# Tails of the output product in pairs, a residual on GpSimd, and tails of w2's transposed product two chunks at a time

## The chip, the cores and the metric

The kernel runs on one core of one Trainium2 chip. The metric is device time in microseconds (us), the median of several executions. A core has a matrix engine (TensorE, "PE" in the profile, with its weight loads as "PEld"), a vector engine (VectorE, "DVE"), an activation engine (ScalarE, "ACT"), a general engine (GpSimd, "POOL") and SyncE ("SP"), which here only issues DMAs. Each engine works through its own instruction list in order; semaphores tie the lists together. DMAs are issued from a queue of SP, ACT or POOL, and a DMA that must wait holds up what stands behind it on that queue. Data lies in SBUF (128 partitions) and, for matmul results, in PSUM, of which the kernel uses eight banks of 128 x 512 float32.

## The reference

The forward pass is a linear-attention block and a gated MLP, each with a layer norm ahead of it and a residual; the program returns the result and the gradients of the input and of five weights. S = 2048 rows, D = 640, 32 heads of 20, hidden size F = 1728. In short:

```python
h  = x + attention(layernorm(x), wqkv, wo)      # linear attention, phi(t) = elu(t) + 1
xn = layernorm(h)
gate = xn @ w1 ;  up = xn @ w3                  # 640 -> 1728
hh = silu(gate) * up
h2 = h + hh @ w2                                # output 0
# backward, from the given gradient g of h2:
ghh = g @ w2.T                                  # 640 -> 1728
g_up, g_gate = ghh * silu(gate), ghh * up * silu'(gate)
grad_w2 = hh.T @ g                              # and so on for w1, w3, wo, wqkv, x
```

All inputs and outputs are bfloat16; products add up in float32.

## The kernel before

F = 1728 is 13 chunks of 128 columns and a tail of 64: `FT = 14`, `FL = 64`. The 2048 rows are handled in `SC = 4` chunks of `W = 512`, each of `TPC = 4` row tiles of 128; `HD = 320` is half of D.

The program runs attention first, then the MLP stage, then the gradient of w2 and the rest of the backward pass. The change touches the MLP stage, and a mask that attention uses.

**The loop of the MLP stage.** For chunk `c` and hidden chunk `fc`, `mlp(c, fc, between)` issues, in this order: five matmuls of 128 x 512 of w2's transposed product for the position two ahead (`mlp_ghh`, `ghh_chunk`, L398 for the tail and L386 through `mm5_to` else); five matmuls of w1 (`gp`); ACT's two sigmoids (L772, L773); five matmuls of w3 (`upp`); ACT's copies of both to SBUF (L779, L783). The copy of L783 needs its `gate` buffer to be free, so the store that reads the buffer's former contents must have landed. At `fc = 13`, where only 64 columns are left of both, `gp` holds w1's and w3's tail together. Two hidden chunks make a pair. `mlp_pair` puts seven VectorE operations of 128 x 1024 on a list, `later` (L808): gate×sig, then hhT, then s2, gate×ghh, two on s2, ghh. Their results go to DRAM: hhT from SP's queue (`hh_d`), the other two from POOL's (`gg_d`, L791). `drain` takes one at a time off the list, four times for each `fc`.

**The tail of w2's transposed product.** At `fc = 13` of the product (issued at `fc = 11` of the loop) the stationary operand has 64 columns. The tail of a chunk is computed as two column halves of the array, one for each 256 rows of the chunk: 10 matmuls of 64 columns by 256 in one PSUM bank, copied by ACT in two steps.

**The output product.** `o2_steps(c)` is a generator: 8 accumulations (4 row tiles, 2 halves of D) of 14 matmuls of 128 x 320 each, L833, 112 in all. The last one of each has 128 rows in the contraction like the others; its lower 64 rows of w2 are zeros (a memset on GpSimd, L881). It yields after each 7 or 8 matmuls. The loop of chunk `c + 1` takes one step for each `fc`; VectorE adds h to each half (L838). Chunk 3's own product runs after the loop, with one entry of `later` drained at each step, and its results are stored from ACT's queue. The next stage's first loads (`load_hh(0)`) and the gradient of w2 (L1025, its tail of column halves L1011) follow.

**The residual.** `f2_at(t)` computes h for row tile `t`: five matmuls of 128 x 320 for each half (L642) and the addition of x. In tiles 5 to 7 (and in the second halves of 0 to 3) TensorE does the addition: one more matmul with the identity (L640), then ACT copies the sum to `x_sb` (L647). Elsewhere VectorE adds from PSUM. `ln2.part` then takes VectorE's statistics of the half (L147), and `f2_hn` normalizes: VectorE's small operations (L150, L153), a power on GpSimd (L154), and a VectorE operation of 128 x 640 (L160). Tiles 4 to 15 are made during chunks 0 to 2, one chunk ahead of their use: tiles 5, 6 and 7 in chunk 0.

**The mask.** `make_mask` fills a block-diagonal mask of 128 x 5 x 7 x 20 with a VectorE memset and two GpSimd selects for each block row; `masked` multiplies by it.

Of the kernel before, what the change touches and what calls it, by code (L numbers as in the profile page):

```python
# [9 lines left out]
P = 128  # L10
# [45 lines left out]
def kernel(  # L56
# [136 lines left out]
    load_x(3, 4)  # L193
    load_x(4, 8)

    mask = cp.tile([P, DT, M_MAX, DH], BF16, name="mask")

    def make_mask(m):
        a, b = M_H[m]
        v = mask[:, m, 0:b - a, :]  # L200
        V.memset(v, 1.0)

        G.affine_select(out=v, in_=v, pattern=[[-DH, b - a], [0, DH]], compare_op=ALU.is_ge, fill=0.0,
                        base=m * P - a * DH, channel_multiplier=1)
        G.affine_select(out=v, in_=v, pattern=[[DH, b - a], [0, DH]], compare_op=ALU.is_gt, fill=0.0,
                        base=a * DH + DH - m * P, channel_multiplier=-1)

    def masked(out, acc, m):

        a, b = M_H[m]  # L210
        V.tensor_tensor(out=out[:, m, a * DH:b * DH].rearrange("p (h e) -> p h e", e=DH),
                        in0=acc.rearrange("p (h e) -> p h e", e=DH), in1=mask[:, m, 0:b - a, :], op=ALU.mult)


    w1 = U2.tile([P, DT, FP], BF16, name="w1", tag="A")
# [171 lines left out]
                     stop=(c == DT - 1))  # L387
        return acc

    def ghh_chunk(n, acc):  # L390

        c, fc = divmod(n, FT)
        if fc == FT - 1:
            gh, hw = ghh[n // 2], W // 2
            G.memset(gh[FL:, 1, :], 0.0)
            for d in range(DT):
                for h in range(2):
                    T.matmul(acc[h * FL:(h + 1) * FL, 0:hw], lhsT=w2T[:, d, fc * P:fc * P + FL],  # L398
                             rhs=g2T[c][:, d, h * hw:(h + 1) * hw], start=(d == 0), stop=(d == DT - 1))
            for h in range(2):  # L400
                A.copy(out=gh[:FL, 1, h * hw:(h + 1) * hw], in_=acc[h * FL:(h + 1) * FL, 0:hw])
            return
        mm5_to(acc, w2T, fc, g2T[c])
# [111 lines left out]
    for t in range(ST):  # L515
        first = None
        if t < RAW:
            first = phi_tiles()
            kh = [ps.tile([P, 512], F32, name="k0", tag="m", bufs=2) for _ in range(2)]

            def act(i, j):
                A.activation(first[i][:, j * HD:(j + 1) * HD], kh[j][:, 0:HD], (AF.Exp, AF.Relu)[i],
                             scale=ln1.rs[:, t:t + 1])

            def between():
                act(0, 0)
                p1_tr(t + 1)
                act(1, 0)
            k = p1_mm(t, D, between, kh)
            act(0, 1)  # L530
            act(1, 1)
        else:
            k = p1_mm(t, D, (lambda: p1_tr(t + 1)) if t + 1 < XT_DMA else None)
        steps = v_steps.get(t, (R,) * len(held))
        for step in steps:
            if step is R:
                held.pop(0)()
            elif step[0] in V_OPS:
                V_OPS[step[0]](step[1])
        phi(k, pk_all[:, t, :], t, first)  # L540
        for when in ("A", "B", "L"):
            for step in steps:
                if step is not R and step[0] == when:
                    p1_norm(step[1])
            if when == "A" and t in QT:
                q_tile(QT.index(t))
        if 3 <= t < 7:
            ghh_chunk(t - 3, ps.tile([P, 512], F32, name="gp", tag="m", bufs=2))
# [80 lines left out]
    ps = pool("pap", space=PSUM)  # L629
    hn, hnT, hhT = {}, {}, {}  # L630

    at_rest = []

    def f2_at(t, tag="at", halves=(0, 1), hold=False):
        for j in halves:
            on_pe = t < 2 * TPC and (t > TPC or (t < TPC and j == 1))
            at = ps.tile([P, 512], F32, name="at", tag=tag, bufs=2)
            xs = x_sb[:, t, j * HD:(j + 1) * HD]
            if on_pe:
                T.matmul(at[:, 0:HD], lhsT=ident[:], rhs=xs, start=True, stop=False)  # L640
            for c in range(DT):
                T.matmul(at[:, 0:HD], lhsT=pqT[:, c, t * P:(t + 1) * P], rhs=Wp[:, c, j * HD:(j + 1) * HD],  # L642
                         start=(c == 0 and not on_pe), stop=(c == DT - 1))

            def rest(at=at, xs=xs, j=j, on_pe=on_pe):
# [109 lines left out]

    def mlp_ghh(n):
        if n < SC * FT:
            ghh_chunk(n, ps.tile([P, W], F32, name="mm", bufs=4))

    AHEAD = 2  # L760

# [36 lines left out]
    def drain(n):  # L798
        for _ in range(min(n, len(later))):
            later.pop(0)()  # L800

    def mlp_pair(c, k, sig, s2, gate, up, gh):

        hh = hhT[c][:, 2 * k:2 * k + 2, :]

        def op(out, a, b, alu=ALU.mult, to=None, r0=0, q=dma):
            def go():
                V.tensor_tensor(out=out, in0=a, in1=b, op=alu)  # L808
                if to is not None:
                    store(to, r0, c, k, out, q)  # L810
            later.append(go)

        sig, s2, gate, up, gh = (x[:] for x in (sig, s2, gate, up, gh))
        op(gate, gate, sig)
        op(hh, gate, up, to=hh_d)
        op(s2, gate, s2)
        op(gate, gate, gh, to=gg_d, r0=F, q=dmaG)
        op(s2, s2, sig, ALU.add)
        op(s2, s2, up)
        op(gh, s2, gh, to=gg_d, q=dmaG)  # L820

    def o2_steps(c, q=dma, tag="o2"):

        jobs = [(i, j, fc) for i in range(TPC) for j in range(2) for fc in range(FT)]
        o2 = {}
        stops = [n * 15 // 2 - 1 for n in range(1, FT)]
        for n, (i, j, fc) in enumerate(jobs):
            if fc == 0:
                o2["ps"] = ps.tile([P, 512], F32, name="o2", tag=tag, bufs=2)
                if j == 0:  # L830
                    t = c * TPC + i
                    o2["sb"] = x_sb[:, t, :] if c == SC - 1 else pf.tile([P, D], BF16, name="h2", bufs=2)[:]
            T.matmul(o2["ps"][:, 0:HD], lhsT=hhT[c][:, fc, i * P:(i + 1) * P],  # L833
                     rhs=w2[:, fc, j * HD:(j + 1) * HD], start=(fc == 0), stop=(fc == FT - 1))
# [43 lines left out]
    pa = pool("pa", "right")  # L878

    w2 = U1.tile([P, FT, D], BF16, name="w2", tag="D")  # L880
    G.memset(w2[64:, FT - 1, :], 0.0)  # L881

    def sides(c):
        side = ({}, {})
# [32 lines left out]
    for c in range(SC):  # L917
# [9 lines left out]
        for fc in range(FT):  # L927
# [15 lines left out]
            if c == 2 and fc == 3:  # L943
# [26 lines left out]
            dmaT(out=hb[b][:, :, a:a + n], in_=hh_d[f0 + a:f0 + a + n, :])  # L970

    load_hh(0)
    for _ in o2_steps(SC - 1, A.dma_start, "at"):
        drain(1)
    pa.release()
    ph.release()
# [166 lines left out]
    def q_parts():  # L1143
# [6 lines left out]
        for m, t0, j in order:  # L1150
# [6 lines left out]
            if (t0, j) == (8, 1):  # L1157
                a, b = M_H[m]
                A.copy(out=two(qp[:, m, :]), in_=acc[m][:, :, 0:HD])
                V.tensor_tensor(out=gz8[:, m, 0:b - a], in0=acc.pop(m)[:, 1, HD + a:HD + b], in1=mask[:, m, 0:b - a, 0],  # L1160
                                op=ALU.mult)
                dmaT(out=QT[:, :, m * P:(m + 1) * P], in_=qp[:, m, :])
            yield
# [343 lines left out]
```

## Time and profile before

| what | value |
|---|---|
| median of 3 runs | 823.68 us (823.57 to 823.91) |
| the profiled execution's span | 821.9 us |
| MLP stage, chunks 0 to 3 and the last output product | about 97 to 342 us of the span |
| TensorE's granted clock | 9 tenths or more in each of 40 slices |
| DMA | 157.26 MB, mean 191 GB/s |

The times are taken around the program, the span is from its first to its last instruction as the hardware profiler saw it; 1.8 us lie between the two. The page's second part cuts the span into 40 slices and prints the busy tenths of each engine:

```profile
PE   8999999999999999999999999999999999999998
PEld 6677544555555555777777777767777777555554
DVE  7869887999898566300057777772681545200000
ACT  7856688665565666011122212222212334211111
POOL 2243333323223212100001111110220000000000
PEclk9999999999999999999999999999999999999999
DMA  9999889696485556999677897258984898885771
```

A slice is 20.5 us. TensorE is busy from end to end; VectorE is nearly as busy as TensorE in slices 5 to 12, which are the MLP stage, and GpSimd has room everywhere.

### The profile page before, as it was taken

To read this page: it belongs to the slowest core of one execution; us is meant where nothing else is said; L and a number is where in the kernel's file an instruction comes from. 1 tells how busy PE (TensorE), PEld (TensorE's weight loads), DVE (VectorE), ACT (ScalarE), POOL (GpSimd) and SP (SyncE) were. 2 spreads that over 40 slices of the span, in tenths; PEclk is the share of its full clock that TensorE was granted. 3 is DMA by queue.
4 is the path that set the end of the run, shared out by engine and by line. 5 is a ranking of instruction groups with operands and counts; after the bars stand their busy time and mean duration, and the time that the engine had idled before them with its cause. 6 is when DMAs were issued, how large, how long until landed. Compare 5 with 4: busy or idle time off the path is not lost.

```text
span 821.9 us, 14179 instructions
## 1 busy us (share of the span) xinstructions
PE 814.4 (99%) x5522; PEld 522.6 (64%) x5549; DVE 453.1 (55%) x961; ACT 325.0 (40%) x609; POOL 133.1 (16%) x194
## 2 busy tenths in 40 slices
PE   8999999999999999999999999999999999999998
PEld 6677544555555555777777777767777777555554
DVE  7869887999898566300057777772681545200000
ACT  7856688665565666011122212222212334211111
POOL 2243333323223212100001111110220000000000
PEclk9999999999999999999999999999999999999999
DMA  9999889696485556999677897258984898885771
GB/s 233 254 279 227 207 234 312 196 242 157 145 213 155 166 181 162 250 241 267 195 170 179 206 204 188 70 113 178 268 216 93 164 200 181 201 199 137 165 170 38
DMA packets 320883, 157.26 MB, mean 191 GB/s; under 512 B 238704, under 2 KB 314064, under 8 KB 320816
## 3 DMA queue, kind: packets, MB, share of 16 engines
q1 hardware_dynamic: 278768, 115.54, 61.3%
q0 software_dynamic: 7328, 24.48, 8.9%
q10 hardware_dynamic: 34720, 16.34, 8.7%
q8 instruction: 43, 0.70, 0.4%
q14 instruction: 24, 0.20, 0.1%
HBM read 47.01 MB, written 51.13 MB: 119 GB/s over the span
## 4 chain that ended last, share of the span: by engine, by line
PE 94%; DVE 2%; ACT 1%; DMA 1%; issue 0%; SPq 0%; POOL 0%; DVEq 0%; ACTq 0%
PE mm L386 20%; PE job L1271 20%; PE ghn L1070 14%; PE gxn L1429 8%; PE o L833 7%; PE gw L1025 7%; PE gwo L1155 3%; PE big L266 3%; PE gr L1127 3%; PE dkv L1375 3%; PE macc L416 2%; PE at L642 2%; DMA wqkv<-in_A_wqkv_dram 1%; PE dkv L1303 1%; DVE st L147 1%; DMA Wp<-pkx 1%
## 5 line engine op out<-in xcount | busy, mean ns | idle before, releaser
L1271 PE MATMUL job<-gb,hnN 128*128 128x432 bf16 (+2 forms) x656 | 117.0, 342 | 0.0
L1070 PEld LDWEIGHTS <-ggb 128*128 128x128 bf16 x864 | 84.5, 98 | 32.8
L1271 PEld LDWEIGHTS <-hnN 128*128 128x128 bf16 x656 | 63.6, 98 | 53.4
L386 PE MATMUL mm<-pqT,w 128*128 128x512 bf16 x397 | 93.1, 379 | 0.5
L386 PEld LDWEIGHTS <-w 128*128 128x128 bf16 x540 | 52.5, 98 | 63.1 <-issue 0.8
L1275 ACT CAST obs<-job 128x432 bf16<-128x432 f32 (+3 forms) x61 | 29.3, 480 | 123.1 <-PE job L1271 123.1
L833 PE MATMUL o<-w,hhT 128*128 128x320 bf16 x448 | 67.7, 299 | 0.1
L1070 PE MATMUL ghn<-w13a,ggb 128*128 128x320 bf16 x448 | 63.5, 299 | 0.0
L1070 PE MATMUL ghn<-w13b,ggb 128*128 128x320 bf16 x416 | 61.4, 299 | 0.0
L386 PE MATMUL mm<-g2T,w2T 128*128 128x512 bf16 x227 | 58.5, 379 | 0.6
L833 PEld LDWEIGHTS <-hhT 128*128 128x128 bf16 x448 | 43.8, 98 | 23.8 <-issue 0.2
L1025 PE MATMUL gw<-g,hb 128*128 128x320 bf16 x416 | 56.8, 299 | 0.0
L1135 POOL TENSOR_TENSOR sz<-Zb,g_h 128x640 f32<-128x640 bf16 x16 | 20.2, 1260 | 198.8 <-DVE g_h L1133 107.7
L1025 PEld LDWEIGHTS <-hb 128*128 128x128 bf16 x416 | 40.6, 98 | 16.0 <-issue 0.3
L1429 PE MATMUL gxn<-wqT,gT 128*128 128x320 bf16 x320 | 48.7, 299 | 0.0
L406 ACT CAST ghh<-mm 128x512 bf16<-128x512 f32 x48 | 28.3, 590 | 44.7 <-PE mm L386 39.0
L772 ACT ACTIVATE sig<-mm 128x512 bf16<-128x512 f32 x56 | 33.9, 605 | 25.1 <-PE mm L386 21.6
L1082 ACT ACTIVATE gs<-ghn 128x640 bf16<-128x640 f32 x16 | 11.2, 703 | 78.9 <-PE ghn L1070 73.4
L386 PEld LDWEIGHTS <-w2T 128*128 128x128 bf16 x260 | 25.4, 98 | 23.3
L266 PEld LDWEIGHTS <-pqT 128*128 128x128 bf16 x320 | 30.6, 98 | 14.4 <-issue 1.7
L1429 PEld LDWEIGHTS <-gT 128*128 128x128 bf16 x320 | 31.3, 98 | 12.2
L266 PE MATMUL big<-wqkv,pqT 128*128 128x320 bf16 x250 | 38.5, 299 | 0.3
(210 smaller groups left out, 1282.3 us busy)
## 6 DMA issues: line engine op xcount, KB each, us to landing
hh_d<-hhT SPq DMA_DIRECT2D x24, 256.0 KB, 2.8
gg_d<-gate POOLq DMA_DIRECT2D x24, 256.0 KB, 4.1
gg_d<-ghh POOLq DMA_DIRECT2D x24, 256.0 KB, 3.5
ggb<-gg_d SPq DMA_DIRECT2D x6, 896.0 KB, 5.4
ggb<-gg_d ACTq DMA_DIRECT2D x6, 832.0 KB, 5.7
out_dram<-obs ACTq DMA_DIRECT2D x39, 108.0 KB, 3.0
x_sb<-in_A_x_dram SPq DMA_DIRECT2D x6, 640.0 KB, 5.4
ggb<-gg_d SPq DMA_DIRECT2D x2, 1728.0 KB, 13.5
```

The lines of the kernel that those rows point to most:

```text
L266: T.matmul(acc, lhsT=pqT[:, c, t * P:(t + 1) * P], rhs=wqkv[:, c, n0:n0 + HD], start=(c == 0), stop=(c == DT - 1))
L386: T.matmul(acc[:], lhsT=w[:, c, fc * P:(fc + 1) * P], rhs=rhs[:, c, :], start=(c == 0), stop=(c == DT - 1))
L406: A.copy(out=ghh[n // 2][:, n % 2, :], in_=acc[:])
L772: A.activation(sig[:, i, :], gp[:], AF.Sigmoid)
L833: T.matmul(o2["ps"][:, 0:HD], lhsT=hhT[c][:, fc, i * P:(i + 1) * P], rhs=w2[:, fc, j * HD:(j + 1) * HD], start=(fc == 0), stop=(fc == FT - 1))
L1025: T.matmul(acc[:, j, 0:HD], lhsT=hb[b][:, t, i * P:(i + 1) * P], rhs=g2[:, t, j * HD:(j + 1) * HD], start=(t == 0), stop=(t == ST - 1))
L1070: T.matmul(acc[:, j, 0:HD], lhsT=ggb[t // 2][:, k, lo:lo + P], rhs=rhs[:, j * HD:(j + 1) * HD], start=(k == 0), stop=(k == NG - 1))
L1127: T.matmul(gr[t][:, j, 0:HD], lhsT=ghT[t][:, c, :], rhs=wT2[:, c, j * HD:(j + 1) * HD], start=(c == 0), stop=(c == DT - 1))
L1155: T.matmul(acc[m][:, j, 0:n], lhsT=r_sb[:, t, m * P:(m + 1) * P], rhs=g_hx[:, t, j * HD:j * HD + n], start=(t == 0), stop=(t == ST - 1))
L1271: T.matmul(acc[:, 0:n], lhsT=lhs[:, t, m * P:(m + 1) * P], rhs=rhs(t), start=(t == 0), stop=(t == ST - 1))
L1275: A.copy(out=ob, in_=acc[:, 0:n])
L1429: T.matmul(acc[:, j, 0:HD], lhsT=g, rhs=wqT[:, k, j * HD:(j + 1) * HD], start=(k == 0), stop=(k == 14))
```

## The change

It has four parts.

1. *Tails of w2's transposed product.* An even chunk computes its own tail and that of the next chunk in one group of 20 matmuls into one PSUM bank; ACT copies the second half to a new tile, `ght2`, from which the odd chunk's two copies read.
2. *Residual of tiles 5, 6 and 7.* The six identity matmuls go. ACT copies the product to a float32 tile `xa`, GpSimd adds x (two additions of 128 x 320 a tile, on the queue that also issues the `gg_d` stores and the power), and the statistics are held back until the end of that `fc`, behind one more drained VectorE operation.
3. *Output product of chunks 2 and 3* (`o2_pairs`). Row tiles `i` and `i + 2` of one half of D share the last step: the tail's 64 contraction rows of tile `i` stand in partitions 0 to 63, those of `i + 2` in 64 to 127, so w2's tail is loaded a second time to the upper partitions (a load of 80 KB more, and the memset goes), and hhT's tail of the last 256 rows is copied there by a DMA of 64 x 256 on SP's queue, as an eighth entry of the list `later`. Tile `i` ends with its tail; tile `i + 2` begins with it. Chunk 2 does this in two groups of four tails, chunk 3 in one group of eight with all eight PSUM banks. The steps yield after each 8 of the 104 full matmuls, so there are 13 yields.
4. *Mask.* It has one element for each head, and `masked` reads it with a broadcast along the 20 columns.

```diff
-    def ghh_chunk(n, acc):
+    def ghh_chunk(n, new_acc):
...
-            for d in range(DT):
+            if c % 2 == 0:
+                src = new_acc()
+                for k in range(2):
+                    for d in range(DT):
+                        for h in range(2):
+                            T.matmul(src[h * FL:(h + 1) * FL, k * hw:(k + 1) * hw], lhsT=w2T[:, d, fc * P:fc * P + FL],
+                                     rhs=g2T[c + k][:, d, h * hw:(h + 1) * hw], start=(d == 0), stop=(d == DT - 1))
+                ghh["next"] = pf.tile([P, hw], BF16, name="ght2")
+            else:
+                src = ghh["next"]
...
+            if c % 2 == 0:
+                A.copy(out=ghh["next"][:], in_=src[:, hw:2 * hw])
...
-            on_pe = t < 2 * TPC and (t > TPC or (t < TPC and j == 1))
+            on_pe = t < TPC and j == 1
+            on_pool = TPC < t < 2 * TPC
...
+                if on_pool:
+                    xa = pf.tile([P, HD], F32, name="xa", tag="h2", bufs=2)
+                    A.copy(out=xa[:], in_=at[:, 0:HD])
+                    G.tensor_tensor(out=xs, in0=xa[:], in1=xs, op=ALU.add)
+                    st_later.append(lambda: ln2.part(x_sb, t, j))
+                    return
...
         op(hh, gate, up, to=hh_d)
+        if c >= SC - 2 and k == FT // 2 - 1:
+            later.append(lambda: dma(out=hh[FL:, 1, W // 2:], in_=hh[:FL, 1, W // 2:]))
...
+    def o2_pairs(c, groups, q):
...
+        def main(i, j, first):
+            for fc in range(lo):
+                T.matmul(accs[i, j][:, 0:HD], lhsT=hhT[c][:, fc, i * P:(i + 1) * P],
+                         rhs=w2[:, fc, j * HD:(j + 1) * HD], start=(first and fc == 0), stop=(not first and fc == lo - 1))
+                done[0] += 1
+                if done[0] % 8 == 0:
+                    yield
...
+        for low, tags in groups:
+            for (i, j), tag in zip(low, tags):
+                acc_of(i, j, tag)
+                yield from main(i, j, True)
+            for (i, j), tag in zip(low, tags[len(low):]):
+                acc_of(i + 2, j, tag)
+                js = slice(j * HD, (j + 1) * HD)
+                for k, first in ((i, False), (i + 2, True)):
+                    r0 = FL * first
+                    T.matmul(accs[k, j][:, 0:HD], lhsT=hhT[c][r0:r0 + FL, lo, k * P:(k + 1) * P],
+                             rhs=w2[r0:r0 + FL, lo, js], start=first, stop=not first)
+            for i, j in low:
+                end(i, j)
+            for i, j in low:
+                yield from main(i + 2, j, False)
+                end(i + 2, j)
...
+        if c == SC - 2:
+            yield from o2_pairs(c, [([(i, 0), (i, 1)], ["o2", "o2", "at", "at"]) for i in range(2)], q)
+            return
+        if c == SC - 1:
+            yield from o2_pairs(c, [([(i, j) for i in range(2) for j in range(2)],
+                                     ["at", "at", "o2", "o2", "mm", "mm", "mm", "mm"])], q)
+            return
...
-    G.memset(w2[64:, FT - 1, :], 0.0)
...
             drain(1)
+            stats_held()
...
-                    dma(out=w2[0:FL, FT - 1, :], in_=B_w2[(FT - 1) * P:F, :])
+                    for r0 in (0, FL):
+                        dma(out=w2[r0:r0 + FL, FT - 1, :], in_=B_w2[(FT - 1) * P:F, :])
```

More of the change, by code (lines that the diff above doesn't have):

```diff
@@ L194 @@
     load_x(4, 8)
-    mask = cp.tile([P, DT, M_MAX, DH], BF16, name="mask")
+    mask = cp.tile([P, DT, M_MAX], BF16, name="mask")
     def make_mask(m):
         a, b = M_H[m]
-        v = mask[:, m, 0:b - a, :]
+        v = mask[:, m, 0:b - a]
         V.memset(v, 1.0)
-        G.affine_select(out=v, in_=v, pattern=[[-DH, b - a], [0, DH]], compare_op=ALU.is_ge, fill=0.0,
+        G.affine_select(out=v, in_=v, pattern=[[-DH, b - a]], compare_op=ALU.is_ge, fill=0.0,
                         base=m * P - a * DH, channel_multiplier=1)
-        G.affine_select(out=v, in_=v, pattern=[[DH, b - a], [0, DH]], compare_op=ALU.is_gt, fill=0.0,
+        G.affine_select(out=v, in_=v, pattern=[[DH, b - a]], compare_op=ALU.is_gt, fill=0.0,
                         base=a * DH + DH - m * P, channel_multiplier=-1)
@@ L211, in masked @@
         V.tensor_tensor(out=out[:, m, a * DH:b * DH].rearrange("p (h e) -> p h e", e=DH),
-                        in0=acc.rearrange("p (h e) -> p h e", e=DH), in1=mask[:, m, 0:b - a, :], op=ALU.mult)
+                        in0=acc.rearrange("p (h e) -> p h e", e=DH), in1=mask[:, m, 0:b - a].unsqueeze(2).to_broadcast([P, b - a, DH]),
+                        op=ALU.mult)
     w1 = U2.tile([P, DT, FP], BF16, name="w1", tag="A")
@@ L395, in ghh_chunk @@
             G.memset(gh[FL:, 1, :], 0.0)
-            for d in range(DT):
-                for h in range(2):
-                    T.matmul(acc[h * FL:(h + 1) * FL, 0:hw], lhsT=w2T[:, d, fc * P:fc * P + FL],
-                             rhs=g2T[c][:, d, h * hw:(h + 1) * hw], start=(d == 0), stop=(d == DT - 1))
+            if c % 2 == 0:
[8 more added lines that the diff above has]
+                src = ghh["next"]
             for h in range(2):
-                A.copy(out=gh[:FL, 1, h * hw:(h + 1) * hw], in_=acc[h * FL:(h + 1) * FL, 0:hw])
+                A.copy(out=gh[:FL, 1, h * hw:(h + 1) * hw], in_=src[h * FL:(h + 1) * FL, 0:hw])
+            if c % 2 == 0:
+                A.copy(out=ghh["next"][:], in_=src[:, hw:2 * hw])
             return
-        mm5_to(acc, w2T, fc, g2T[c])
+        acc = mm5_to(new_acc(), w2T, fc, g2T[c])
         if n % 2 == 0:
@@ L547 @@
         if 3 <= t < 7:
-            ghh_chunk(t - 3, ps.tile([P, 512], F32, name="gp", tag="m", bufs=2))
+            ghh_chunk(t - 3, lambda: ps.tile([P, 512], F32, name="gp", tag="m", bufs=2))
         m_part(0, M0.get(t, ()))
@@ L630, with stats_held @@
     hn, hnT, hhT = {}, {}, {}
-    at_rest = []
+    at_rest, st_later = [], []
+    def stats_held():
+        while st_later:
+            st_later.pop(0)()
     def f2_at(t, tag="at", halves=(0, 1), hold=False):
         for j in halves:
-            on_pe = t < 2 * TPC and (t > TPC or (t < TPC and j == 1))
+            on_pe = t < TPC and j == 1
+            on_pool = TPC < t < 2 * TPC
             at = ps.tile([P, 512], F32, name="at", tag=tag, bufs=2)
@@ L643, in f2_at, with rest @@
                          start=(c == 0 and not on_pe), stop=(c == DT - 1))
-            def rest(at=at, xs=xs, j=j, on_pe=on_pe):
+            def rest(at=at, xs=xs, j=j, on_pe=on_pe, on_pool=on_pool):
+                if on_pool:
[4 more added lines that the diff above has]
+                    return
                 if on_pe:
@@ L757, in mlp_ghh @@
         if n < SC * FT:
-            ghh_chunk(n, ps.tile([P, W], F32, name="mm", bufs=4))
+            ghh_chunk(n, lambda: ps.tile([P, W], F32, name="mm", bufs=4))
     AHEAD = 2
@@ L820, in mlp_pair, with acc_of, end, o2_steps @@
         op(gh, s2, gh, to=gg_d, q=dmaG)
-    def o2_steps(c, q=dma, tag="o2"):
+    def o2_pairs(c, groups, q):
+        accs, done, sb = {}, [0], {}
+        lo = FT - 1
+        def acc_of(i, j, tag):
+            accs[i, j] = ps.tile([P, 512], F32, name="o2", tag=tag, bufs=4 if tag == "mm" else 2)
+        def main(i, j, first):
[5 more added lines that the diff above has]
+                    yield
+        def end(i, j):
+            t, js = c * TPC + i, slice(j * HD, (j + 1) * HD)
+            if c == SC - 1:
+                sb[i] = x_sb[:, t, :]
+            elif j == 0:
+                sb[i] = pf.tile([P, D], BF16, name="h2", bufs=2)[:]
+            V.tensor_tensor(out=sb[i][:, js], in0=accs.pop((i, j))[:, 0:HD], in1=x_sb[:, t, js], op=ALU.add)
+            if j == 1:
+                q(out=out0S[:, t, :], in_=sb[i])
+        for low, tags in groups:
[14 more added lines that the diff above has]
+                end(i + 2, j)
+    def o2_steps(c, q=dma):
+        if c == SC - 2:
+            yield from o2_pairs(c, [([(i, 0), (i, 1)], ["o2", "o2", "at", "at"]) for i in range(2)], q)
+            return
+        if c == SC - 1:
+            yield from o2_pairs(c, [([(i, j) for i in range(2) for j in range(2)],
+                                     ["at", "at", "o2", "o2", "mm", "mm", "mm", "mm"])], q)
+            return
         jobs = [(i, j, fc) for i in range(TPC) for j in range(2) for fc in range(FT)]
@@ L828, in o2_steps @@
             if fc == 0:
-                o2["ps"] = ps.tile([P, 512], F32, name="o2", tag=tag, bufs=2)
+                o2["ps"] = ps.tile([P, 512], F32, name="o2", bufs=2)
                 if j == 0:
-                    t = c * TPC + i
-                    o2["sb"] = x_sb[:, t, :] if c == SC - 1 else pf.tile([P, D], BF16, name="h2", bufs=2)[:]
+                    o2["sb"] = pf.tile([P, D], BF16, name="h2", bufs=2)[:]
             T.matmul(o2["ps"][:, 0:HD], lhsT=hhT[c][:, fc, i * P:(i + 1) * P],
@@ L972 @@
     load_hh(0)
-    for _ in o2_steps(SC - 1, A.dma_start, "at"):
+    for _ in o2_steps(SC - 1, A.dma_start):
         drain(1)
@@ L1159, in q_parts @@
                 A.copy(out=two(qp[:, m, :]), in_=acc[m][:, :, 0:HD])
-                V.tensor_tensor(out=gz8[:, m, 0:b - a], in0=acc.pop(m)[:, 1, HD + a:HD + b], in1=mask[:, m, 0:b - a, 0],
+                V.tensor_tensor(out=gz8[:, m, 0:b - a], in0=acc.pop(m)[:, 1, HD + a:HD + b], in1=mask[:, m, 0:b - a],
                                 op=ALU.mult)
```

## The prediction

> **What bounds the kernel now.** I read the page's first part (busy time by engine), then its chain of waits, then the windows and the timelines of the places that the change touches.
>
> ```profile
> PE 814.4 (99%) x5522; PEld 522.6 (64%) x5549; DVE 453.1 (55%) x961; ACT 325.0 (40%) x609; POOL 133.1 (16%) x194
> ...
> PE 94%; DVE 2%; ACT 1%; DMA 1%; issue 0%; SPq 0%; POOL 0%; DVEq 0%; ACTq 0%
> ```
>
> TensorE is busy for 99% of the span and is 94% of the chain. So a matmul taken away is worth its own pitch at once, and a wait put in front of a matmul costs its whole length. The averages hide how near the other engines are, so I cut the MLP stage into windows (start and end; length; busy us of PE, PEld, DVE, ACT, POOL with instruction counts; PE clock; DMA share; GB/s):
>
> ```profile
> 110.00:120.00 10.00, 9.95 (x51) 4.99 (x51) 8.86 (x17) 6.66 (x13) 5.05 (x7) 1.00 0.90 254
> 158.00:203.50 45.50, 45.29 (x255) 24.53 (x258) 44.16 (x95) 25.41 (x48) 14.39 (x20) 1.00 0.72 199
> 324.00:331.00 7.00, 6.97 (x52) 4.91 (x51) 5.80 (x12) 2.25 (x4) 1.29 (x3) 1.00 0.46 151
> ```
>
> The clock is 1.00, TensorE has no gap worth a name. In chunk 0 (first row) DMA is at 0.90; in chunk 1 (second) VectorE is at 44.16 of 45.50, so it can hardly give way. Whatever the change makes late shows on TensorE only where the slack runs out; I look for those places.
>
> **Part 1, matmuls taken away.** Prices: an output-product matmul of 320 columns is 0.136 us (2.04/15 in the chain), one of 512 columns 0.216 us (5 between 322.90 and 323.98). A group of 64-column tails (rows of the timeline and of the chain: start, us, engine, what, count; later also idle time and its releaser):
>
> ```profile
> 130.31 2.32 PE L386 MATMUL mm<-pqT,w 128*128 128x512 bf16 x10
> 132.56 0.74 PE L398 MATMUL mm<-g2T,w2T 128*64 128x256 bf16 x10
> ...
> 203.51 2.04 PE o L833 x15
> ...
> 394.97 2.29 PE gt L1011 x32
> ```
>
> Ten matmuls from 130.31 end at 132.47, the group starts at 132.56 and the next matmul follows at 133.23: 0.67 for five pairs of 0.108 (256 columns), so about 0.1 before and 0.1 behind, 0.2 a group. L1011 shows that column halves run in pairs: 32 in 2.29, 0.14 a pair.
> - w2's transposed product: the same matmuls in two groups instead of four: 2 × 0.2 = −0.40.
> - Residual: six identity matmuls of row tiles 5, 6, 7 go: 6 × 0.136 = −0.82.
> - Output product's tails: no row of before has two 64-*row* halves together. Lower bound of the gain: they run one by one, the count stays 16, and three switches of 0.2 are paid: +0.6. Upper: pairs at no switch: 8 × 0.136 = −1.09. I take pairs with a switch of 0.2 a group, as for column halves, the nearest row. Chunk 3: 8 × 0.136 = 1.09 becomes 4 × 0.14 + 0.2 = 0.76; chunk 2, twice: 0.54 becomes 0.48. Sum −0.45.
>
> Together −1.67. The Trainium skill ("TensorE: Matmul & The Clock Gate", Part 3) states that matmuls in different row groups start a few ns apart and run at once, which is the value taken; no run here shows it yet.
>
> **Part 2, what is hidden.** The mask of 7 instead of 140 elements a partition: GpSimd's selects stand before its 7.67 us of idle time ahead of 57.03, so nothing is gained; the broadcast operand keeps VectorE's element count. Taken 0, bounds −0.1 and +0.2 (one masked product, 0.3 us, late by half). The extra w2 load (80 KB) and the two SBUF copies of hhT's last 64 rows (64x256) are on SP's queue, behind the hh_d stores and ahead of later out_0 stores; the copy is wanted 52 matmuls, 7.1 us, after chunk 3's product begins, against 3.9 us from issue to landing for the hh_d stores (median of the DMA issues between 100 and 160). Taken 0, bounds 0 and +0.3. The two ACT copies more are 0.4 each (two 128x320 in 0.76 at 120.19) where ACT is 56% busy (25.41/45.50): 0. The memset of w2's pad (0.62 on POOL): 0.
>
> **Part 3, the end of chunk 3's loop.** The steps of the output product end after 8 instead of 7 or 8 matmuls, so the step after the loop has no matmul left. Between the last gate product and the first matmul that needs the last pair's hhT stood 22 + 12 = 34 matmuls, 4.62 us; now 8 + 12 = 20, 2.72 us. What they cover:
>
> ```profile
> 322.90 1.24 PE L386 MATMUL mm<-hnT,w 128*128 128x512 bf16 x5
> ...
> 324.18 0.60 ACT L772 ACTIVATE sig<-mm 128x512 bf16<-128x512 f32 x1 [1.04 <-PE mm L386]
> 325.87 0.58 ACT L783 CAST gate<-mm 128x512 bf16<-128x512 f32 x1
> ...
> 326.49 0.69 DVE L808 TENSOR_TENSOR gate<-gate,sig 128x1024 bf16<-128x1024 bf16 x1 [1.02 <-ACT gate L783]
> 327.21 0.69 DVE L808 TENSOR_TENSOR hhT<-gate,up 128x1024 bf16<-128x1024 bf16 x1
> ```
>
> The gate product ends at 323.98, hhT at 327.90: 3.92 later, all of it a chain ACT, ACT, DVE, DVE that the change leaves alone. Matmul 13 waits 3.92 − 2.72 = 1.20. One matmul on, (0,1) takes the PSUM tile that chunk 2's last tile leaves, and that addition (0.44) now stands right behind hhT on VectorE: 327.90 + 0.44 = 328.34, 4.36 behind 323.98, against 2.72 + 1.20 + 0.14 = 4.06: another 0.30. Before paid 0.06 there (gap at 330.96). Sum +1.44; bounds 1.2 (only the first wait) and 2.1 (one more VectorE operation of 0.69 between).
>
> **Part 4, GpSimd's additions in chunk 0.** Price: two in 1.53, so 0.765 each, against nothing on VectorE before (TensorE added).
>
> ```profile
> 63.60 1.53 POOL L358 TENSOR_TENSOR pr<-hx,Zb 128x320 f32<-128x320 bf16 x2 [1.26 <-DVE rden L365]
> ...
> 110.06 0.71 POOL L791 DMA_DIRECT2D gg_d<-ghh  x1 [1.03 <-DVE ghh L808]
> 110.28 0.88 DVE L147 BATCH_NORM_STATS2 st<-x_sb 128x6 f32<-128x320 bf16 x2
> 113.06 0.69 DVE L808 TENSOR_TENSOR gate<-gate,ghh 128x1024 bf16<-128x1024 bf16 x1
> 114.30 0.74 POOL L791 DMA_DIRECT2D gg_d<-gate  x1 [1.68 <-ACT up L779]
> 119.71 0.58 ACT L783 CAST gate<-mm 128x512 bf16<-128x512 f32 x1 [2.61 <-DMA gg_d<-gate]
> 121.13 1.24 PE L386 MATMUL mm<-g2T,w2T 128*128 128x512 bf16 x5
> ```
>
> Tile 5: the additions stand on POOL behind the issue that ends at 110.77, so they end at 112.30; the two statistics wait for them on VectorE and end near 112.8, not 111.16. hhT goes ahead of them now, but behind them stand the norm's small operations, GpSimd's power (0.88 from 111.74), hn that waits for it, and gate×ghh behind hn: 113.06 + 1.64 = 114.7, with rounding 114.4 to 114.9: +1.35 to +1.85, and with it the issue at 114.30. Who waits: ACT's gate copy at 119.71 (its buffer is read by that store, idle 2.61), which frees at 120.29 the PSUM tile that TensorE wants at 121.13. Slack 0.84, of which 0.54 goes since TensorE comes four identity matmuls earlier: 0.30. So a stall of 1.05 to 1.55, with up to 0.3 behind it at the next up product: 1.85 at most. At the least 0: this store took 5.35 from issue to landing, the median of all gg_d stores is 4.1, and 1.35 − 1.25 is under the slack; against it, the median between 100 and 160 is 5.3. Taken the middle, +0.95. Tiles 6 and 7 have 1 to 4 us of slack at each wait. Chunk 1's VectorE (1.34 idle, less 0.66 of TensorE time gone there): 0, upper bound +0.5.
>
> A rule speaks against this part: the Trainium skill ("SBUF — State Buffer", Who interferes with whom) has GpSimd and VectorE lock one port pair for a whole instruction when VectorE has two SBUF inputs. Its sign is in the trace: a 640-wide scalar operation took 1.86 at 60.67 beside GpSimd products, and 0.32 alone at 75.92. By the rule six additions could hold VectorE 6 × 0.765 = 4.6 us more, and the sum would rise by up to that, less what VectorE's idle times in the chunk (1.59, 0.71, 1.37, 1.74 behind 110) take; by the order used here VectorE stands in the statistics meanwhile, one input each, and nothing is added.
>
> **Sum.** −1.67 + 1.44 + 0.95 = +0.72 against the profiled 821.9, so 822.6. The median, 823.68, is 1.8 above that span (time around it, unchanged): 824.4.
>
> **The rivals.**
> - *Cover holds*: the store lands at the median time, no stall in chunk 0. For it: landings differ by over 1 us. 823.68 − 1.67 + 1.44 = 823.45; with tails at no switch (−0.64) and 1.2 at the loop's end, 822.6; and if the chain at 323.98 were shorter too, under 822.0. Against: the chain is ACT and DVE time, not DMA.
> - *VectorE held by GpSimd (slower)*: in chunk 0 each addition stretches a VectorE operation, as 1.86 for 0.32 at 60.67. For it: VectorE 8.86 of 10.00 busy there; against: the order puts it in the statistics. From 114.9 on, each us of lateness of gate×ghh goes one to one to TensorE, from 0.9 on the time is over 825.33; with two of the six stretched by 1.5, 824.4 + 0.9 to 2.4: 825.4 to 826.8.
> - *Row halves run one by one*: +0.6 in place of −0.45: 824.4 + 1.05 = 825.5. The change then doesn't do what it says. Only the column halves of L1011 speak against it.
>
> **Numbers.** A measurement of this kernel tells 0.2% (1.65 us) from no change, so "same" is 822.03 to 825.33. Likeliest 0.52 (its own range 823.5 to 825.3), cover holds 0.25 (0.10 of it under 822.03), held VectorE 0.15, one by one 0.08 (half under 825.33). Faster 0.10; slower 0.15 + 0.04, and 0.03 for the likeliest's upper bounds: 0.22; same 0.68. Range 822.3 to 826.0: some 0.07 are left out below and 0.1 above.
>
> **What would show it.** Right: no identity rows of tiles 5 to 7; two L398-like groups of 20; the four pairs of chunk 3 in some 0.55 us; TensorE waits of 1.2 and 0.3 behind the last gate product, released by DVE; ACT's wait for gg_d<-gate near 120 longer by over 1 us, TensorE idle behind it. Wrong: no gap at the loop's end (another order on DVE); tail pairs at 0.27 each; VectorE operations of over 1 us in chunk 0; TensorE gaps between 158 and 203 (VectorE has become the bound).

## The result and the profile after

The changed kernel takes 827.11 us (median of 5 runs, 825.62 to 828.34) against 823.68 us before; the ratio is 1.0036, with a 95% interval of 1.0024 to 1.0048. Measured once more beside other kernels it took 826.11 against 823.80, ratio 1.0022 (1.0010 to 1.0034). It is slower, by 3.4 and 2.3 us between the medians, and both medians lie above the forecast range of 822.3 to 826.0, the second by 0.1.

The page of the changed kernel, busy time by engine and the shares of the chain of waits:

```profile
PE 813.6 (99%) x5516; PEld 521.0 (63%) x5543; DVE 454.2 (55%) x961; ACT 324.9 (39%) x611; POOL 135.3 (16%) x199
...
PE 84%; DVE 8%; DMA 3%; issue 3%; ACT 1%; POOL 1%; SPq 0%; DVEq 0%; POOLq 0%; ACTq 0%
```

TensorE has less to do (813.6 for 814.4), and the span is longer (824.8 for 821.9). VectorE is now 8% of the chain, DMA 3%: TensorE waits. Where, the windows tell (start and end; length; busy us of PE, PEld, DVE, ACT, POOL with instruction counts; PE clock; DMA share; GB/s). Before:

```profile
125.00:158.00 33.00, 32.79 (x172) 16.40 (x175) 28.27 (x53) 26.11 (x50) 10.73 (x16) 1.00 0.91 269
...
324.00:345.00 21.00, 20.97 (x155) 14.99 (x154) 10.36 (x20) 2.25 (x4) 2.96 (x6) 1.00 0.94 216
```

After:

```profile
125.00:158.00 33.00, 31.11 (x166) 15.32 (x168) 27.44 (x51) 23.80 (x48) 12.94 (x19) 1.00 0.88 263
158.00:203.00 45.00, 44.50 (x245) 24.18 (x248) 43.90 (x96) 26.11 (x50) 13.91 (x21) 1.00 0.77 201
324.00:345.00 21.00, 19.81 (x140) 12.86 (x138) 13.30 (x24) 4.41 (x8) 3.64 (x6) 1.00 0.77 174
```

TensorE stands still for 1.9 us in the rest of chunk 0 (33.00 − 31.11) and for 1.2 us at the end of chunk 3. A finer account comes from the start times of the same matmuls in two traces. The table gives how much later they start than before, in the first profile of the changed kernel and in that of its second measurement:

| matmul | start before | first | second |
|---|---|---|---|
| residual product, tile 0, second half | 90.27 | +0.72 | −0.05 |
| residual product, tile 7 | 124.5 | +0.11 | −0.58 |
| residual product, tile 8 (chunk 1) | 157.8 | +2.75 | +1.79 |
| residual product, tile 11 | 191.62 | +3.20 | +2.27 |
| residual product, tile 12 (chunk 2) | 218.1 | +2.42 | +1.49 |
| residual product, tile 15 | 256.2 | +2.42 | +1.49 |
| gradient of w2, first | 342.37 | +3.08 | +2.15 |

The first row is a wait for a DMA transpose in attention (1.10 us at 31.99). The changed kernel's second profile doesn't have it, and of the kernels below only the one without the residual has it (1.28), so it isn't counted to the change. From tile 0 to tile 7 five of the six identity matmuls are won; the sixth (0.14) stands behind that row. Between tiles 7 and 8 stand +2.64 and +2.37; 0.55 of it is chunk 1's tails, done early, and the sixth identity matmul, which is gone there, hides 0.14 of waits: 2.2 and 2.0 are waits. Chunk 1 adds 0.45, its missing tail group gives 0.78 back, and from tile 15 to the end stands +0.66, the last cover against the gains of chunks 2 and 3.

The timeline of the changed kernel, chunk 0 (start, us, engine, what, count, idle before and its releaser):

```profile
111.10 2.41 DVE L828 TENSOR_TENSOR hhT<-gate,up 128x1024 bf16<-128x1024 bf16 x1
113.43 0.87 DVE L147 BATCH_NORM_STATS2 st<-x_sb 128x6 f32<-128x320 bf16 x2
116.15 0.68 DVE L828 TENSOR_TENSOR gate<-gate,ghh 128x1024 bf16<-128x1024 bf16 x1
...
111.49 1.46 POOL L663 TENSOR_TENSOR x_sb<-xa,x_sb 128x320 bf16<-128x320 f32 x2
117.13 0.74 POOL L811 DMA_DIRECT2D gg_d<-gate  x1 [1.38 <-DVE gate L828]
122.09 0.71 POOL L811 DMA_DIRECT2D gg_d<-gate  x1 [1.61 <-ACT ghh L415]
...
120.28 0.58 ACT L803 CAST gate<-mm 128x512 bf16<-128x512 f32 x1 [0.22 <-DMA gg_d<-gate]
129.96 0.58 ACT L803 CAST gate<-mm 128x512 bf16<-128x512 f32 x1 [2.86 <-DMA gg_d<-gate]
...
130.59 1.24 PE L387 MATMUL mm<-g2T,w2T 128*128 128x512 bf16 x5 [1.22 <-ACT gate L803]
```

Two things differ from the forecast. hhT, which took 0.68, took 2.41 beside GpSimd's additions, and gate×ghh started at 116.15, not at 114.4 to 114.9 (0.7 of this is attention's wait; the second profile has 115.45, and the same 2.41). VectorE has no pause between this row and 122.87, so the lateness is handed on whole to the next pair. And the gate copy that TensorE waits for is not the forecast one (119.71 before, here 120.28, idle only 0.22) but the next but one, at 129.96: its store went out at 122.09, 3.1 us later than before (119.01), of which 0.7 is attention's wait (121.39 in the second profile, 2.4 later), and landed 7.8 us later. The rows of before at that place, of GpSimd, ACT and TensorE:

```profile
119.01 0.71 POOL L791 DMA_DIRECT2D gg_d<-gate  x1 [1.61 <-issue]
125.12 0.74 ACT L783 CAST gate<-mm 128x512 bf16<-128x512 f32 x1
129.23 1.24 PE L386 MATMUL mm<-g2T,w2T 128*128 128x512 bf16 x5
```

There the store landed at 124.7, the copy had 0.4 us to spare, and TensorE wanted its PSUM tile 3.5 us after the copy. The DMA issues of that moment, in before's trace (last number: us from issue to landing):

```profile
gg_d<-gate POOLq DMA_DIRECT2D x1, 256.0 KB, 5.7
```

and in the changed kernel's:

```profile
gg_d<-gate POOLq DMA_DIRECT2D x1, 256.0 KB, 7.8
```

The end of chunk 3's loop, TensorE's timeline in the changed kernel:

```profile
326.88 1.24 PE L387 MATMUL mm<-hnT,w 128*128 128x512 bf16 x5
327.96 2.88 PE L854 MATMUL o<-w,hhT 128*128 128x320 bf16 x20
331.94 5.86 PE L854 MATMUL o<-w,hhT 128*128 128x320 bf16 x40 [1.10 <-DVE hhT L828]
337.72 0.72 PE L879 MATMUL o<-w,hhT 64*128 64x320 bf16 x8
338.37 7.24 PE L854 MATMUL o<-w,hhT 128*128 128x320 bf16 x52
```

20 matmuls at 0.136 end at 330.68; the next starts at 331.94: a wait of 1.26, and one matmul on another of 0.26 (331.94 to 332.33, less one pitch). The eight tails take their place from 337.63 to 338.37, 0.74 for 1.09 before; the trace's single records start in twos, 0.003 apart, each pair 0.133 after the last, with 0.1 before and 0.1 behind the group.

### The profile page after: what moved, and what is told of

Same layout as the page of the kernel before. It is cut to its first block, busy times and chain, and to the rows that moved or that the text cites. A ratio compares the mean times of both kernels' runs of the same rounds, so it can differ in the third digit from the quotient of the medians.

```text
span 824.8 us, 14177 instructions
## 1 busy us (share of the span) xinstructions
PE 813.6 (99%) x5516; PEld 521.0 (63%) x5543; DVE 454.2 (55%) x961; ACT 324.9 (39%) x611; POOL 135.3 (16%) x199
## 4 chain that ended last, share of the span: by engine, by line
PE 84%; DVE 8%; DMA 3%; issue 3%; ACT 1%; POOL 1%; SPq 0%; DVEq 0%; POOLq 0%; ACTq 0%
PE job L1343 19%; PE ghn L1142 14%; PE mm L387 11%; PE gxn L1501 8%; PE gw L1097 7%; PE o L854 3%; PE big L267 3%; PE gwo L1227 3%; PE gr L1199 3%; PE dkv L1447 3%; PE macc L425 2%; PE o L904 2%; DMA gg_d<-gate 2%; DVE s L828 1%; PE at L656 1%
## 5 line engine op out<-in xcount | busy, mean ns | idle before, releaser
L1343 PEld LDWEIGHTS <-g 128*128 128x128 bf16 x320 | 31.0, 98 | 11.6
L803 ACT CAST gate<-mm 128x512 bf16<-128x512 f32 x56 | 33.9, 605 | 7.8 <-DMA gg_d<-gate 7.7
```

The costliest lines, as they stand in the source:

```text
L803: A.copy(out=gate[:, i, :], in_=gp[:])
L1343: T.matmul(acc[:, 0:n], lhsT=lhs[:, t, m * P:(m + 1) * P], rhs=rhs(t), start=(t == 0), stop=(t == ST - 1))
```

## The experiments

All kernels compute the whole reference. Each was timed in 11 or 12 runs (the one with the statistics not held in 5) beside the kernel before, whose median was 824.16 in the first four, 824.01 in the next four, 823.80 in the next four and 823.87 in the last two. Runs of one kernel lie 2 to 6 us apart, and each trace is of one run, which can lie far from the median.

| run | median, us | ratio to before | 95% interval |
|---|---|---|---|
| residual alone | 825.64 | 1.0017 | 1.0007 to 1.0027 |
| paired tails alone | 825.42 | 1.0019 | 1.0010 to 1.0028 |
| mask alone | 823.74 | 0.9996 | 0.9983 to 1.0008 |
| group of 20 tails alone | 823.89 | 0.9996 | 0.9984 to 1.0007 |
| residual, third gate buffer | 823.83 | 0.9996 | 0.9984 to 1.0008 |
| residual, statistics not held | 827.36 | 1.0044 | 1.0031 to 1.0056 |
| residual on VectorE | 824.10 | 1.0001 | 0.9989 to 1.0013 |
| no residual, cover by yields | 825.51 | 1.0018 | 1.0008 to 1.0029 |
| changed kernel again | 826.11 | 1.0022 | 1.0010 to 1.0034 |
| no residual | 825.39 | 1.0019 | 1.0003 to 1.0036 |
| no residual, full cover | 824.03 | 1.0004 | 0.9989 to 1.0018 |
| residual, load of g earlier | 824.93 | 1.0007 | 0.9995 to 1.0019 |
| both waits taken away | 824.53 | 1.0007 | 0.9998 to 1.0016 |
| changed kernel, full cover | 823.83 | 1.0001 | 0.9990 to 1.0012 |

**The four parts one by one.** Each is the diff's part put into the kernel before, with nothing else changed: the residual (`f2_at`, `stats_held`), the paired tails (`o2_pairs`, w2's second load, hhT's copy), the mask, and the group of 20 tails (`ghh_chunk`).

> The kernel before with the residual of tiles 5 to 7 on GpSimd alone. Theory 1 (the loss is the lateness in chunk 0: hhT beside the additions took 2.41 us instead of 0.68, the gate stores go out 3 us late, ACT's gate copy and then TensorE wait): -0.82 for six identity matmuls, +2.2 and +0.45 for the waits seen at 129 to 142 and at 192 in the changed kernel: 825.5 us, between 824.8 and 827. Theory 2 (the loss sits elsewhere, in the start stage or at the end of chunk 3's loop): 823.7 - 0.82 + at most 0.95 as forecast: 822.9 to 823.8.

> The kernel before with the paired tails of the output product of chunks 2 and 3 alone. As forecast: -0.45 for the tails, +1.44 for the shorter cover behind the last gate product: 824.7 us. If the row halves run one by one: 825.7. If the cover held and the pairs ran: 823.2.

> The kernel before with the small mask alone. Theory 1: nothing, 823.7 us (823.3 to 824.2 as the kernel before itself). Theory 2: the wait of 1.1 us for a DMA transpose at 32 us of the changed kernel's trace comes with the mask: 824.4 to 825.

> The kernel before with the tails of w2's transposed product two chunks at a time alone. As forecast: two group switches of 0.2 us less: 823.3 us. If the odd chunks, which now have 0.66 us less of TensorE work, are bound by VectorE there: 823.7 to 824.2.

Measured against 824.16: +1.48, +1.26, −0.42 and −0.27. The residual and the paired tails each cost more than they win; the intervals of the other two include no change. The sum is +2.05, close to the changed kernel's second measurement (+2.31). In the paired tails alone the trace has, besides the waits above, 0.58 us at the first matmul of w2's gradient for a PSUM tile; the changed kernel, whose tiles turn in another order, doesn't have it.

The timeline of the residual alone, chunk 0:

```profile
110.21 0.69 DVE L819 TENSOR_TENSOR hhT<-gate,up 128x1024 bf16<-128x1024 bf16 x1
111.55 0.49 DVE L147 BATCH_NORM_STATS2 st<-x_sb 128x6 f32<-128x320 bf16 x1 [0.64 <-POOL x_sb L654]
114.60 0.69 DVE L819 TENSOR_TENSOR gate<-gate,ghh 128x1024 bf16<-128x1024 bf16 x1
...
120.54 0.71 POOL L802 DMA_DIRECT2D gg_d<-gate  x1 [1.61 <-ACT ghh L406]
...
128.50 0.58 ACT L794 CAST gate<-mm 128x512 bf16<-128x512 f32 x1 [2.95 <-DMA gg_d<-gate]
```

Here hhT isn't stretched, VectorE waits in the statistics, and gate×ghh starts at 114.60, inside the forecast 114.4 to 114.9. Still the store of 120.54 lands 7.9 us later and ACT waits 2.95, and TensorE behind it:

```profile
129.13 1.24 PE L386 MATMUL mm<-g2T,w2T 128*128 128x512 bf16 x5 [0.73 <-ACT gate L794]
```

So the wait comes without the stretch; a store 1.5 us late (120.54 for 119.01) with a landing of 7.9 us is enough. The trace is of the shortest of 11 runs (824.22), and between tiles 7 and 8 it has 1.3 us of waits where the changed kernel has 2.2 and 2.0. How much of this difference is the stretch isn't shown, since no run takes it alone out of the changed kernel.

**Taking the wait away.** `gate` gets a third buffer (the small mask and one shared tile make room).

```diff
-        return pa.tile([P, 2, W], BF16, name=name, bufs=2)
+        return pa.tile([P, 2, W], BF16, name=name, bufs=3 if name == "gate" else 2)
```

> The residual on GpSimd alone (as in the first experiment, 825.64 there against 824.16 of before in the same call) with a third buffer for gate; the small mask and one shared 64-byte tile make the room. Theory 1 (the path is gate x ghh late, its store late and landing late, ACT's gate copy waits for the buffer, TensorE waits for ACT): the wait goes, what remains is -0.82 and at most 0.5 elsewhere: 823.2 to 823.8 where before has 824.0. Rival (VectorE as a whole is behind, TensorE waits for it by other ways too): 825 and more.

823.83, where the residual alone had 825.64. TensorE's timeline at the place of the wait:

```profile
127.07 2.32 PE L389 MATMUL mm<-pqT,w 128*128 128x512 bf16 x10
129.23 1.24 PE L389 MATMUL mm<-g2T,w2T 128*128 128x512 bf16 x5
130.31 2.32 PE L389 MATMUL mm<-pqT,w 128*128 128x512 bf16 x10
```

Ten matmuls of 0.216 from 127.07 end at 129.23, and the next start there: no wait, although the store of this pair (issued 121.44) took 8.0 us to land in this trace too. So the wait at 129 was a wait for the buffer. By the medians nearly all of the loss goes with it, though this run has the small mask besides, which alone came to −0.42 with an interval that includes no change. The trace, of a run of 824.69, shows another wait further on, for ACT's copy of ghh, which itself waits 2.79 us for a `gg_d` store of ghh:

```profile
146.78 1.24 PE L389 MATMUL mm<-pqT,w 128*128 128x512 bf16 x5 [0.50 <-ACT ghh L409]
```

So in some executions the lateness can still cost something at another buffer.

**Held statistics, and the port.** The statistics of tiles 5 to 7 go back to their place right behind the additions, so hhT of tile 5 stands behind them and not beside the additions.

```diff
-                    st_later.append(lambda: ln2.part(x_sb, t, j))
+                    ln2.part(x_sb, t, j)
```

> The residual on GpSimd alone, but the statistics are not held back: hhT stands behind them again and not beside the additions. If the stretched hhT (2.41 us instead of 0.68) is what makes gate x ghh late: hhT at 0.68, gate x ghh some 0.9 earlier, 824.7 us. If VectorE's wait for the additions counts and the stretch only fills it: 825.6 as with the statistics held.

827.36, worse by 1.7 than with the statistics held. hhT takes 0.68, but VectorE idles instead; its timeline:

```profile
111.86 0.50 DVE L147 BATCH_NORM_STATS2 st<-x_sb 128x6 f32<-128x320 bf16 x1 [1.25 <-POOL x_sb L654]
114.96 0.68 DVE L819 TENSOR_TENSOR gate<-gate,ghh 128x1024 bf16<-128x1024 bf16 x1
...
123.89 0.49 DVE L147 BATCH_NORM_STATS2 st<-x_sb 128x6 f32<-128x320 bf16 x1 [2.93 <-POOL x_sb L654]
```

At tile 6 it waits 2.93 for the additions, and in the same trace, of the longest of 5 runs, TensorE waits 1.62 us at 122.71 and 1.37 at 145.95 for ACT's gate copy. Neither theory had this: holding the statistics is right, and it is the wait for GpSimd's result that has to be covered. On the stretch this run says nothing, since the residual alone, with the statistics held, has hhT at 0.69 as well.

**The residual on VectorE.** VectorE adds from PSUM in tiles 5 to 7, with the statistics held.

```diff
-                    xa = pf.tile([P, HD], F32, name="xa", tag="h2", bufs=2)
-                    A.copy(out=xa[:], in_=at[:, 0:HD])
-                    G.tensor_tensor(out=xs, in0=xa[:], in1=xs, op=ALU.add)
+                    V.tensor_tensor(out=xs, in0=at[:, 0:HD], in1=xs, op=ALU.add)
```

> The residual of tiles 5 to 7 on VectorE, from PSUM, instead of GpSimd; the six identity matmuls gone as well. Theory 1: six additions of 0.44 us more on VectorE (2.6 us in a chunk with 5.4 us of idle time behind 110 us), no wait for GpSimd: 824.0 - 0.82 + 0 to 1.0 = 823.2 to 824.2. Rival (any VectorE time more in this chunk goes onto the path): 825.5 and more.

824.10: level with before, 1.5 better than on GpSimd. Six additions of 0.44 on the busier engine cost less than six on the idle one. In its trace VectorE doesn't wait for the sums, and the gate store goes out 4.3 us after tile 6's residual product starts, against 4.7 in the residual alone and 2.8 before. The store still took 8.0 us to land, and TensorE waits 0.38 for the gate copy. That the spared wait for another engine's answer makes the whole difference is argued, not shown.

**The load that the store meets.** In before, the gate store was issued at 119.01, 0.3 us behind SP's transposed load of g for chunk 1; with the residual on GpSimd it is 0.9 behind. The load was moved from `fc` 6 to 3.

```diff
-            if fc == (6, 3, 3)[min(c, 2)] and c < SC - 1:
+            if fc == (3, 3, 3)[min(c, 2)] and c < SC - 1:
```

> The residual on GpSimd alone, with the transposed load of g for chunk 1 issued three steps of fc earlier (10 us), away from tile 6's gate store, which in the first experiment's trace took 7.9 us to land instead of 5.7 and ended TensorE's wait at 129 us. If the DMA queueing behind this load stretches the store: landing near 5.5, 0.9 to 1.3 us won of 825.6: 824.3 to 824.7. Rival (w2's loads or the lateness alone): 825.6; a load that collides with an earlier store: 826 and more.

824.93, between the two. The store, issued at 120.76, is as late as in the residual alone, but it lands in 6.2 us; ACT's wait is 1.31, not 2.95, and TensorE has no wait at 129. The DMA issues at that store, then ACT's and TensorE's timelines of this kernel:

```profile
gg_d<-gate POOLq DMA_DIRECT2D x1, 256.0 KB, 6.2
```

```profile
127.08 0.58 ACT L794 CAST gate<-mm 128x512 bf16<-128x512 f32 x1 [1.31 <-DMA gg_d<-gate]
...
142.29 2.32 PE L386 MATMUL mm<-pqT,w 128*128 128x512 bf16 x10 [0.89 <-ACT gate L794]
```

The last row is a new wait, for a later gate copy. Between tiles 7 and 8 the waits come to 1.1 us, against 1.3 in the residual alone, so in these two traces the wait has moved more than gone, and the medians (0.7 apart, with intervals that overlap) don't decide what the move was worth.

The other traces show more of this landing. Where the residual is as before, the same store, 0.1 to 0.5 us behind the load, took 5.5 to 5.9 us in five traces (before, paired tails alone, group of 20 alone, and the two covers without the residual), but 8.2 with the mask alone (0.43 behind) and 7.9 with no residual (0.38 behind). So neither the residual nor the distance behind the load decides the landing, and what does is open. In those last two traces TensorE has no wait between 125 and 158. At 129, then, a long landing alone costs nothing, a late issue with a landing of 6.2 costs nothing, and the two together cost a wait.

**The cover behind the last gate product.** First without the residual, and with it as it was:

> The changed kernel without the residual part, the other three parts as they are. If the parts add up: 824.0 + 1.26 - 0.42 - 0.27 = 824.6, some 1.5 under the changed kernel. If the residual hurts more together with the group of 20 tails that stands 4 us behind its last tile: 824.6, and 2.5 under the changed kernel. Rival (the residual isn't the larger part): 826.

> The changed kernel once more, beside the next three on one chip. 827.1 as before if the four parts hurt each other (alone they came to +1.48, +1.26, -0.42 and -0.27 against before, together +2.05); 826.1 if they only add up.

825.39 and 826.11. The residual is worth 0.7 between these medians, less than the 1.48 found alone; the intervals (0.33% and 0.24% wide) allow both. The profile without the residual has lost 1.4 us already in attention, by the same DMA transpose as above; whether other runs behind this median have that wait isn't known. Then the cover put back, at first by the yields alone:

```diff
-                if done[0] % 8 == 0:
+                if done[0] % 7 == 0 and done[0] <= 13 * 7:
```

> The changed kernel without the residual part, and chunk 2's output product yields after each 7 matmuls 13 times, so that 13 + 7 matmuls stand behind the last gate product and 32, not 20, ahead of the first that needs its hhT. If the short cover costs 1.44 as forecast: 824.0 - 0.40 - 0.45 + 0.1 = 823.2 us. If the loss of the paired tails (+1.26 alone) comes from elsewhere, 824.4 to 824.8.

825.51, not the 823.2 of the theory, and the trace says why:

```profile
324.42 2.88 PE L854 MATMUL o<-w,hhT 128*128 128x320 bf16 x20
328.80 3.42 PE L854 MATMUL o<-w,hhT 128*128 128x320 bf16 x24 [1.50 <-DVE h L866]
```

With 91 = 7 × 13 matmuls done, the generator yields just ahead of the addition that frees row tile (3,0)'s PSUM tile, so the addition lands on VectorE behind hhT, and chunk 3's first matmul waits for it. The cover was there; the wait had a new releaser. With the PSUM tiles changed over as well:

```diff
-                                     ["at", "at", "o2", "o2", "mm", "mm", "mm", "mm"])], q)
+                                     ["o2", "o2", "at", "at", "mm", "mm", "mm", "mm"])], q)
```

> As the last, with the cover behind the last gate product put back in full: chunk 2's product yields after each 7 matmuls, and chunk 3's first two accumulations take the PSUM tiles that were free long before (o2, not at), so that no addition on VectorE stands between. The earlier try left a wait of 1.50 for that addition. Theory: waits of 1.26 and 0.30 go: 824.6 - 1.5 = 823.1. Rival (the time isn't won, it waits for hhT's last pair anyway): 824.6.

824.03, and TensorE's timeline has no wait any more, 72 matmuls in 9.94:

```profile
325.27 9.94 PE L854 MATMUL o<-w,hhT 128*128 128x320 bf16 x72
335.14 0.72 PE L879 MATMUL o<-w,hhT 64*128 64x320 bf16 x8
```

1.36 less than without the cover, for a forecast 1.44. But it isn't under before, although all that is left are gains. In the profile of this kernel a wait stands at the beginning of chunk 2:

```profile
207.83 1.46 PE L387 MATMUL mm<-pqT,w 128*128 128x512 bf16 x6 [1.47 <-DMA pqT<-hn]
```

TensorE comes earlier there, since chunk 1 has lost its tail group, and the normalized last tile, which VectorE makes late, isn't transposed yet. The waits there differ from profile to profile, and no run took VectorE's load off chunk 1, so that this wait eats the gain of the 20 tails in general is argued, not shown.

**Both at once.**

> The changed kernel with the full cover behind the last gate product alone, the residual on GpSimd as it is. If the losses add up: 826.1 - 1.4 = 824.7 us. If the time won there goes into another wait of the full change: 826.

> The residual on GpSimd and the paired tails, with both waits taken away: a third gate buffer, and the full cover behind the last gate product (the group of 20 tails is left out to make room). If these two waits are the whole loss, the gains are left: 823.8 - 0.82 - 0.45 + 0.5 (waits at 131 and 192 that stay) = 823.0 us, under the kernel before. If something else in the full change costs as much: 824.5 and more.

The changed kernel with the full cover takes 823.83, level with before: 2.3 less than the changed kernel, more than the 1.4 expected, and what the other 0.9 is stays open; the lowest of its 11 runs is 823.21, that of the changed kernel's 12 is 824.82, 1.6 apart. Its profile, of one of its longest runs, still has a wait of 1.45 for ACT's gate copy at 130.14. With both waits taken away and the group of 20 left out it is 824.53, 1.5 more than the theory had: TensorE's waits in its trace, of its longest run, are 1.7 us for hn at the beginning of chunk 0, 0.8 in two waits for ACT's copy of up and, as in the paired tails alone, 0.6 us for a PSUM tile at the first matmul of w2's gradient. The waits that were aimed at are gone, but not all of the loss: that these two waits are the whole of it isn't shown. No version here is clearly faster than the kernel before.

## Why the forecast was wrong

- *Chunk 0: the step that failed.* "Tiles 6 and 7 have 1 to 4 us of slack at each wait" put tile 6 at nothing. The slack was as large as I said: 3.9 us for tile 6's store (0.4 to the copy, 3.5 from there to TensorE). But I set no lateness against it, and it met three pieces: the store was 2.4 later (tile 5's delay, handed on by a VectorE without a pause), its landing 2.1 to 2.2 longer, and TensorE 0.7 earlier, 5.2 to 5.3 together. The +0.95 was put on the copy before it, at a landing of 5.35 to 4.1; that store landed in 3.1 and cost nothing. Between matched matmuls the stall is 1.4 and 1.5 us at 130 and 0.4 at the next up product, and with smaller ones behind it 2.2 and 2.0 for the rest of the chunk, where the sum had +0.95. By the medians the residual alone costs 1.48 + 0.82 = 2.3; its trace, of its shortest run, shows 1.3 there and 0.3 in chunk 1.
- *"VectorE stands in the statistics meanwhile, one input each, and nothing is added."* Wrong for tile 5 in the full change: the order, as I had written it, has hhT ahead of the statistics, and hhT was held until both of tile 5's additions had ended (111.49 + 1.46 = 112.95): +1.73. Two of the six additions did what the rival of a held VectorE says of all. For two the rival had 825.4 to 826.8, where the second median lies; that is luck, since the residual alone loses 1.48 with no stretch in its trace. The Trainium skill's rule on the port pair ("SBUF — State Buffer", Who interferes with whom: an operation with two SBUF inputs contends with a GpSimd operation that reads SBUF) speaks of this very operation; I weighed it against the statistics and not against what the reordering puts beside the additions. The row that I took for its sign, 1.86 at 60.67, is of an operation with one SBUF input and so no row of that rule. In tiles 6 and 7 VectorE did stand in the statistics.
- *Gains.* Identity matmuls 0.136 each, right (−0.53 to −0.69 seen for five of them from tile 0 to 7, beside small waits; −0.82 by the price for six). Group of 20: −0.40 forecast; by the rows 0.55 more in the even chunk and 0.77 less in the odd one, 0.22 a pair of chunks, −0.44, of which its own trace has −0.31 left from tile 7 to the gradient of w2. Paired tails: −0.45 forecast, −0.48 measured (0.34 in chunk 3; four tails in 0.47 for 0.54, twice). The row halves do run side by side, so that rival is out.
- *End of chunk 3's loop.* Right in mechanism, place and size: 1.2 + 0.3 forecast, 1.26 + 0.26 measured, released by hhT and then by the addition. Putting the cover back won 1.36.
- *Chunk 1.* Taken 0 with an upper bound of 0.5; 0.45 and 0.48 at 191.62 in the two profiles, 0.3 in the residual alone. But the paired tails alone have 0.46 there too, and they change next to nothing ahead of it: VectorE has 1.34 us left in 45, and the wait need not come from the change.

With these in place the sum is −0.82 − 0.44 − 0.48 + 1.5 + 2.2 + 0.45 = +2.4 for the first profile and, with 2.0 and 0.48, +2.2 for the second. Behind tile 0 the two profiles have lost 2.4 and 2.2; the waits are read off these same profiles, so only the gains are tested by this. The second median is 2.3 above before, the first 1.1 more. Of that its profile, of a run (826.48) below its median, shows 0.7 in attention; what the rest is stays open.

## What to carry to other kernels

Set the whole lateness against a slack: late issue, longer landing, and the time by which the waiting engine now comes earlier. And take a store's landing by its range, not its median: here the same store took 5.5 to 9.7 us behind the same load, and a delay of 1.5 us became 3.7. When work moves to an idle engine, count the wait for its answer on the busy engine that stands behind it; here adding on the busy one was cheaper. And whoever takes filler out from behind a last product should look first at what that filler covered: the paired tails won 0.5 and uncovered 1.5.

## What was not expected of the hardware

- A 128x1024 VectorE product with two SBUF inputs took 2.41 us beside two GpSimd additions in four profiles (the changed kernel twice, the same with the full cover, and the kernel with both waits taken away), and 0.69 in three others with the residual part (alone, with the third buffer, with the load moved), where it overlapped the same additions by 0.25 us. In the first group the product was recorded 0.38 to 0.39 us ahead of the first addition, in the second 0.44. Though recorded first it was held back; what decides isn't settled.
- Matmuls of 64 rows in the two halves of the array start 0.003 us apart, 0.133 a pair of 320 columns, with 0.19 of switching a group, as for column halves.
- One and the same 256 KB store, issued 0.1 to 0.5 us behind a transposed load, took from 5.5 to 9.7 us to land (5.7 in before, 9.7 with the statistics not held, 0.36 behind), and 7.8 to 8.0 at 0.9 behind. The gate store of the pair before it took 3.1 in the changed kernel and 5.3 in before.
